# Attention with decay and a mixture of experts on one core: the decay of a second block moved to TensorE, a fetch moved ahead of the last features, and a new table of steps

## The chip, the cores and the metric

One core of a Trainium2 chip runs the whole program in one launch. The metric is device time in microseconds (us), the median of several runs. The engines are named as in the profile: PE is TensorE (PEld its weight loads), DVE is VectorE, ACT is ScalarE, POOL is GpSimd, SP is SyncE, whose queue issues most DMAs.

## The reference

Attention with a causal mask and a decay from cumulated gates, then a mixture of 8 experts, of which each row uses one:

```python
scores = (1 / sqrt(D)) * q @ k.T                  # B=8, H=8, S=576, D=64
cum = cumsum(log(clip(f, 1e-4, 1)))
scores = where(causal, -1e9, scores + cum[:, None] - cum[None, :])
attn = exp(scores - max(scores)); attn /= sum(attn) + 1e-9
x = (attn @ v).transpose(...).reshape(4608, 512)
e = argmax(x @ w_gate)                            # one expert for each row
out[row] = gate * sigmoid(x @ w_output_gate)[e] * (relu(x @ w1[e]) @ w2[e])
```

## The kernel before, in words

**Attention** works on 32 pairs of heads (u = 0 to 31), both heads of a pair side by side on the partitions. A row's maximum is found ahead of its scores, by a product of 16-bit halves in four parts (`maxsteps`): the full block (rows 384 to 511, 512 columns), a mixed part (the third block, 384 columns, and the first, 128), the second block (rows 128 to 255, 256 columns) and the rest (the last 64 rows of both heads). All four write the one PSUM tile `mx`, so each product waits until DVE has reduced the part before it. From pair 2 on, the decay of all blocks but the first is not in the product: a DVE operation (L294, `CUSTOM_DVE_ANT_0`, one for each head) adds it from the tile `wide` and takes the maximum. Where the decay is in the product (`Eq`, `Ek`), a plain reduction (L279) is enough.

The maxima are turned on PE (`mt`), copied to rows (`mts`, L353) and stored into `Eq` by DMA (`max_put`). Then PE makes the scores `sc` in three groups for each head, ACT takes the exponentials (L378, tile `p`), and the rest of each exponential against its 16-bit part is a subtract (`plo`, L380) on POOL. PE multiplies `p` and `plo` with the values (`av`), DVE and ACT normalise (L483 to L499). Other subtracts of the same kind are those of the values V (`Vs`, L124 called from `load_v`: part 0 on POOL, part 1 on DVE) and of the features (`feats`, L124 and L523 on DVE). All these DVE subtracts have both inputs in SBUF.

**Routing** (`route`) runs for one batch, that is four pairs, at a time: a product `lg`, a chain of small DVE operations, ranks `rk`, and then 4 or 5 indirect DMAs that scatter rows into the table (`tbl`, L643) on POOL. A batch with an odd number has 5 tiles, one with an even number 4. `hold_early` (L549 to L552) reserves places of an early expert; it uses the same PSUM bank as `mt`, `lg`, `rk` and the rest's scores `rs`.

**Order.** All of attention is issued in an order written out by the table `OFF`: the loop of `attention()` counts steps s, six to a pair; each kind of work has an offset there, and `order` says in which order the kinds of one step are issued. Each engine works through its own queue in that order. `'hold'` has the steps of `hold_early`, `'v'` those of `load_v`, `'first'` the step of the first pair's maxima.

**Experts.** For each, W1 and W2 come in 8 pieces each by DMA (`fetch_w1`, `fetch_w2` on SP's queue) and are split into a 16-bit part (ACT) and a rest; `up_products` makes `hp` (L909), `up_split` its two halves (L918, L919), `down` makes `y` (L937 to L939). The first expert begins with three tiles of rows that are known early. In its loop over fc, the features of the last batch half (`feats(NQ - 1)`) are cast, subtracted, transposed by DMA and stored.

Of the kernel before, what the change touches and what calls it, by code (L numbers as in the profile page):

```python
# [50 lines left out]

OFF = {'lead': 3, 'crow': -12, 'clear': 33, 'clearstep': 12, 'prefill': -12, 'fetch': -21, 'spread': -19, 'end': 204, 'max': (-15, -13, -11, -10), 'pair': -8, 'mturn': -7, 'rows': -6, 'put': -4, 'rscore': 2, 'rexp': 3, 'first': -9, 'av': ((6, 8, 8), (9, 10, 10)), 'fetch_v': -24, 'v': ((-16, -8, -15), (-10, -1, -17)), 'feats0': 20, 'feats1': 22, 'fturn': 22, 'fturnstep': 2, 'fout': 32, 'route': 46, 'rank': 6, 'w1r': [169, 170, 171, 175, 176, 177, 181, 182], 'w1': [174, 175, 176, 179, 181, 183, 185, 187], 'w2r': [183, 184, 185, 186, 187, 188], 'hold': (160, 188), 'ids1': 192, 'gather': 172, 'ids': 7, 'gturn': 6, 'route_last': 200, 'nsum': (9, 11), 'nrec': (10, 12), 'nx': (10, 13), 'nrest': (11, 14), 'mv': ['xr', 'v0', 'sm'], 'begin': -18, 'wg': -4, 'fetch_v/1': -10, 'dve': [181, 183, 185, 187, 189, 191], 'w1pool': [0, 1, 2, 3, 4, 5, 6, 7], 'order': 'scores put nrec reduce max spread tick feats1 rows v0 nsum fout nx tick v1 fetch_v feats0 exps extra pair tick mturn av rexp fturn nrest fetch route rscore tick maxrest'}
MV = OFF['mv']
ENGINES = {mybir.EngineType.PE, mybir.EngineType.Activation, mybir.EngineType.DVE, mybir.EngineType.Pool,
           mybir.EngineType.SP}
# [7 lines left out]
def _attn_moe(ctx, tc, qk, vm, f, wg, w1, w2, out):  # L65
    nc = tc.nc
# [8 lines left out]
    crow = dr.tile([3, B * H, S], F16, name="crow")  # L75
# [76 lines left out]
    order = actx.enter_context(ExitStack())  # L152
# [101 lines left out]
    def maxsteps(u):  # L254

        t = st[u]
        Ku, Qu = upper(t["K"]), upper(t["Q"])
        nR = t["nR"] = a.tile([P, NW], F32, name="nR", bufs=3)
        w = HU * NC
        nW = nR[:, 0:w].rearrange("p (i c) -> p i c", i=HU)  # L260

        def few(x, i, sl):

            return x[i * D:(i + 1) * D - 1, sl]

        def block(m, o, c):
            n = (c + 1) * P
            q = slice(c * P, n)
            decay = [(lambda i: part(m, i, o, n), lambda i: few(t["Eq"], i, q), lambda i: few(t["Ek"], i, slice(0, n)),
                      False, False)]  # L270
            return [(lambda i: part(m, i, o, n), lambda i: Qu[rows(i), q], lambda i: Ku[rows(i), 0:n], True, False),
                    *([] if "wide" in t and c else decay),
                    (lambda i: part(m, i, o + n - P, P), lambda i: pick[rows(i), 0], lambda i: negm[rows(i), 0],
                     False, False),
                    (lambda i: part(m, i, o + n - D, D), lambda i: pick[rows(i), 1], lambda i: negm[rows(i), 1, D:],
                     False, True)]

        def red(o, x):
            nc.vector.tensor_reduce(o, x, axis=AX.X, op=ALU.max)  # L279

        def part(m, i, o, n):
            return m[i][:, o:o + n] if isinstance(m, list) else m[:, i, o:o + n]

        def most(m, o, c):
            n = (c + 1) * P
            if "wide" not in t or not c:
                if isinstance(m, list):
                    for i in range(HU):
                        red(nW[:, i, c:c + 1], part(m, i, o, n))
                else:  # L290
                    red(nW[:, :, c], m[:, :, o:o + n])
                return
            for i in range(HU):
                nc.vector.tensor_tensor_reduce(out=spare[:, 0:n], in0=part(m, i, o, n), in1=t["wide"][:, i * S:i * S + n],  # L294
                                               scale=1.0, scalar=-3e38, op0=ALU.add, op1=ALU.max,
                                               accum_out=nW[:, i, c:c + 1])

        def mtile():
            return ps.tile([P, 2, 512], F32, name="mx", bufs=1)

        def full():
            m = mtile()
            heads(block(m, 0, 3))
            yield
            most(m, 0, 3)

        def mixed():
            m = [ps.tile([P, 512], F32, name="av", bufs=2) for _ in range(HU)] if u < 2 else mtile()
            heads(block(m, 0, 2))
            heads(block(m, 384, 0))  # L310
            yield
            most(m, 0, 2)
            most(m, 384, 0)

        def second():
            m = [ps.tile([P, 512], F32, name="sc", bufs=3) for _ in range(HU)] if u < 1 else mtile()
            heads(block(m, 0, 1))
            yield
            most(m, 0, 1)

        def rest():
            m = mtile().rearrange("p b n -> p (b n)")[:, 0:S]
            q = slice(SM, S)
            for sl in (slice(0, SM), q):
                own = sl is q
                heads([(lambda i: m[rows(i), sl], lambda i: Qu[rows(i), q], lambda i: Ku[rows(i), sl], True, False),
                       (lambda i: m[rows(i), sl], lambda i: few(t["Eq"], i, q), lambda i: few(t["Ek"], i, sl),
                        False, not own)])
            heads([(lambda i: m[rows(i), q], lambda i: pick[rows(i), 0, 0:SR], lambda i: negm[rows(i), 0, 0:SR],
                    False, True)])  # L330
            yield
            red(nR[:, w:w + 1], m)

        return [full(), mixed(), second(), rest()]
# [316 lines left out]
    NF = FF // P  # L651
# [15 lines left out]
    W1, W1r, W2r = [], {}, []  # L667

    def fetch_w2(we, fc):
        raw = ar.tile([P, DM], F32, name="w2r", bufs=6)  # L670
        nc.sync.dma_start(raw, we[fc])
        return raw
# [194 lines left out]
    def split_w2(raw, eng):  # L867
        h = m2.tile([P, DM], F16, name="w2h", bufs=16)
        l = m2.tile([P, DM], BF16, name="w2l", bufs=16)
        nc.scalar.copy(out=h, in_=raw)  # L870
        eng.tensor_tensor(l, raw, h, op=ALU.subtract)
        return h, l
# [29 lines left out]
    def up_products(w1s, x, tiles, fc):  # L902
        xT = x[1]
        wh, wl = w1s[fc]
        hp = [pm.tile([P, 512], F32, name=f"hp{j}", bufs=2) for j in range(len(tiles))]
        for k in range(ND):
            for i, (w, j) in enumerate(((wh, 0), (wh, 1), (wl, 0))):
                for m, (t0, t1) in zip(hp, tiles):
                    nc.tensor.matmul(m[:, 0:(t1 - t0) * P], w[:, k], xT[:, t0:t1, k // 2, j, k % 2],  # L909
                                     start=k == 0 and i == 0, stop=k == ND - 1 and i == 2)  # L910
        return hp

    def up_split(hp, h, tiles, fc):
        hh, hl = h
        for m, (t0, t1) in zip(hp, tiles):
            sl = slice(t0 * P, t1 * P)
            m = m[:, 0:(t1 - t0) * P]
            nc.scalar.activation(out=hh[:, fc, sl], in_=m, func=AF.Relu)  # L918
            nc.vector.scalar_tensor_tensor(hl[:, fc, sl], m, 0.0, hh[:, fc, sl],  # L919
                                           op0=ALU.max, op1=ALU.subtract)  # L920
# [41 lines left out]
    x = st["early"]  # L962
    x1 = (st["ids"], m2.tile([P, CT, 2, 2, DM // P // 2, P], F16, name="xT", bufs=1))
    first = [(0, ET)]
    late_rows = [(ET, CT)]
    with tc.manual_schedule(engines=ENGINES):
# [3 lines left out]
        h = hidden()  # L970
        W2, W1b, W2b = [], [], []
        for fc in range(NF):
            if fc == 1:
                for part in range(2):
                    feats(NQ - 1, part)
                    for t in ((0,), (2, 4))[part]:
                        feats_turn(NQ - 1, t)
                feats_out(NQ - 1)
            up_split(up_products(W1, x, first, fc), h, first, fc)
            W2.append(split_w2(W2r[fc], nc.vector))  # L980
            if len(W2r) < NF:
                W2r.append(fetch_w2(w2[0], len(W2r)))
        W1r = [fetch_w1(m2, w1[1], fc, 8) for fc in range(NF)]
        for t in range(ET):
            gather_turn(x1, t, (ET + t) % CT)
        W2r = [fetch_w2(w2[1], fc) for fc in range(6)]
# [36 lines left out]
        W2r = [fetch_w2(w2[EE], fc) for fc in range(6)]  # L1023
# [9 lines left out]
        W2 = []  # L1033
# [11 lines left out]
        W1, x = W1c, x2  # L1045

        halves = [(0, CT // 2), (CT // 2, CT)]
        for e in range(EE, E):
# [9 lines left out]
            h = hidden()  # L1058
# [8 lines left out]
            if more:  # L1067
                W2r = [fetch_w2(w2[e + 1], fc) for fc in range(6)]
# [5 lines left out]
            if more:  # L1074
                W1, W2, x = W1n, W2n, xn

    with tc.For_i(0, nsl, 1) as i:
# [4 lines left out]
        x = gather(m2, tbl[bass.ds(bi, P)], 1)  # L1082
        h = up(weights(load_w1, w1[bass.ds(ei, 1)].rearrange("a f p k n -> (a f) p k n")), x, [(0, 1)])
# [46 lines left out]
```

## Time and profile before

| | |
|---|---|
| median of 3 runs | 808.67 us (808.04 to 808.94) |
| profiled execution | 803.02 us, span 801.3 us |
| granted TensorE clock, mean over the span | 0.976 |
| PE busy | 749.1 us (93%), 8635 products |
| POOL busy | 483.9 us (60%) |
| DVE busy | 368.9 us (46%) |
| ACT busy | 341.8 us (43%) |
| custom max operations (L294) on DVE | 100.0 us, 180 rows |
| DMA | 121.44 MB, 152 GB/s |

The table is a whole-span mean over stages. Attention fills about the first 371 us, where DVE's and POOL's busy shares in slices are mostly 0.7 to 0.9; the experts fill the rest, where PE is busy without a break and DVE is mostly idle. A timeline row gives the start, the duration, the engine, the line, the operation with output and inputs, how many were merged, and in brackets the idle time before it with what ended it.

### The profile page before, as it was taken

The page shows a single profiled execution, that of the slowest core. Times are in us where ns is not written, and L with a number is a line of the kernel's source. Part 1 is how long each engine was busy: PE and PEld are TensorE (multiplying, and loading weights), DVE is VectorE, ACT ScalarE, POOL GpSimd, SP SyncE. Part 2 cuts the span into 40 slices and gives each one's busy share as a digit, 9 for nine tenths or more (in the row PEclk, how much of TensorE's full clock was granted, in tenths as well). Part 3 has the DMA queues.
Part 4 walks back from the last instruction along what each step waited for, and adds up shares of the span by engine and source line. Part 5 has one row for each costly group of instructions (what it writes and reads, how often), then busy time and mean ns, then how long its engine had stood idle before and what let it go on. Part 6 is the DMA issues. An engine that isn't in the chain of part 4 may idle for free. (4 is left out here: it accounts for less than half of the span.)

```text
span 801.3 us, 21234 instructions
## 1 busy us (share of the span) xinstructions
PE 749.1 (93%) x8635; PEld 489.4 (61%) x8635; DVE 368.9 (46%) x982; ACT 341.8 (43%) x817; POOL 483.9 (60%) x505
## 2 busy tenths in 40 slices
PE   3899998999899989979799999999999999999996
PEld 2577776776577667657354667557466474564752
DVE  7576787787778886795352152102011020120210
ACT  2456664565455563565342434324233233333211
POOL 9768787797768786684162477464473654736001
PEclk9999999999899998998899999999999999999998
DMA  5546669788877976699956929458462593542001
GB/s 184 168 128 167 179 156 148 182 173 180 141 168 172 155 172 138 146 181 199 210 162 148 285 85 228 135 178 182 159 143 94 172 215 101 154 126 80 10 14 44
DMA packets 136180, 121.44 MB, mean 152 GB/s; under 512 B 95310, under 2 KB 104910, under 8 KB 136080
## 3 DMA queue, kind: packets, MB, share of 16 engines
q1 hardware_dynamic: 128528, 101.14, 55.3%
q0 software_dynamic: 7552, 18.92, 7.9%
q8 instruction: 68, 1.11, 0.6%
q14 instruction: 32, 0.26, 0.2%
HBM read 81.63 MB, written 20.48 MB: 127 GB/s over the span
## 5 line engine op out<-in xcount | busy, mean ns | idle before, releaser
L380 POOL TENSOR_TENSOR plo<-p 128x512 f16<-128x512 f32 x186 | 194.3, 1057 | 77.4 <-ACT p L378 74.7
L919 DVE SCALAR_TENSOR_TENSOR hl<-hp,hh 128x384 f16<-128x384 f32 (+1 forms) x128 | 60.8, 491 | 296.4 <-ACT hh L918 296.4
L909 PE MATMUL hp<-xT,w1h 128*128 128x256 f16 (+1 forms) x1024 | 188.0, 299 | 0.1
L378 ACT ACTIVATE p<-sc 128x512 f32<-128x512 f32 x192 | 110.6, 594 | 61.4 <-PE sc L252 60.7
L252 PE MATMUL sc<-qk 64*128 64x64 f32 (+5 forms) x642 | 131.8, 480 | 0.0
L942 POOL DMA_INDIRECT out_dram<-ys,ids x40 | 40.2, 1004 | 143.6 <-ACT ys L941 97.3
L294 DVE CUSTOM_DVE_ANT_0 spare<-mx,wide 128x512 bf16<-128x512 f32 (+1 forms) x180 | 100.0, 556 | 57.5 <-PE mx L252 54.3
L937 PE MATMUL y<-w2h,hh 128*128 128x512 f16 x320 | 122.3, 382 | 4.2 <-ACT w2h L870 4.2
L909 PEld LDWEIGHTS <-w1h 128*128 128x128 f16 x1024 | 100.1, 98 | 40.5 <-issue 0.3
L938 PE MATMUL y<-w2l,hh 128*128 128x512 bf16 x320 | 122.1, 382 | 0.1
L939 PE MATMUL y<-w2h,hl 128*128 128x512 f16 x320 | 122.1, 382 | 0.0
L909 PE MATMUL hp<-xT,w1l 128*128 128x384 f16 (+1 forms) x512 | 121.9, 299 | 0.0
L918 ACT ACTIVATE hh<-hp 128x384 f16<-128x384 f32 (+1 forms) x128 | 50.7, 435 | 121.5 <-PE hp L909 120.6
L941 ACT ACTIVATE ys<-y,ids 128x512 f32<-128x512 f32 x40 | 27.5, 687 | 152.2 <-issue 94.7
L663 POOL TENSOR_TENSOR w1l<-w1r,w1h 128x512 bf16<-128x512 f32 x52 | 59.5, 1156 | 47.2 <-ACT w1h L662 42.6
L252 PEld LDWEIGHTS <-pick 64*128 64x128 bf16 (+1 forms) x1152 | 59.4, 98 | 41.9 <-issue 25.2
L252 PE MATMUL mx<-qk 64*64 64x64 bf16 (+2 forms) x374 | 57.2, 310 | 27.5 <-DVE nR L279 14.6
L452 PE MATMUL av<-Vs,p 128*128 128x65 f16 x640 | 72.0, 196 | 2.5 <-ACT xr L499 2.5
L454 PE MATMUL av<-Vs,plo 128*128 128x65 f16 x640 | 70.9, 194 | 0.5 <-POOL plo L380 0.5
L453 PE MATMUL av<-Vs,p 128*128 128x64 bf16 x640 | 71.3, 197 | 0.0
L452 PEld LDWEIGHTS <-p 128*128 128x128 bf16 x640 | 59.5, 98 | 7.4 <-issue 0.5
L453 PEld LDWEIGHTS <-p 128*128 128x128 bf16 x640 | 60.8, 99 | 2.4 <-issue 2.4
(158 smaller groups left out, 1404.0 us busy)
## 6 DMA issues: line engine op xcount, KB each, us to landing
qk<-in_qk_dram SPq DMA_DIRECT2D x32, 576.0 KB
w1r<-in_w_dram SPq DMA_DIRECT2D x64, 256.0 KB
w2r<-in_w_dram SPq DMA_DIRECT2D x64, 256.0 KB
v<-in_vm_dram SPq DMA_DIRECT2D x16, 576.0 KB
wide<-crow SPq DMA_DIRECT2D x30, 288.0 KB
xbuf<-x SPq DMA_DIRECT2D x16, 512.0 KB
Eq<-mts SPq DMA_DIRECT2D x64, 0.1 KB
xbuf<-x SPq DMA_DIRECT2D x16, 64.0 KB
```

Of the source, the lines that this page charges most:

```text
L252: nc.tensor.matmul(dst(i), w(i), x(i), start=start, stop=stop)
L294: nc.vector.tensor_tensor_reduce(out=spare[:, 0:n], in0=part(m, i, o, n), in1=t["wide"][:, i * S:i * S + n], scale=1.0, scalar=-3e38, op0= ...
L378: nc.scalar.activation(out=f32, in_=src, func=AF.Exp, scale=0.125)
L380: eng.tensor_tensor(lo, f32, upper(f32), op=ALU.subtract)
L452: nc.tensor.matmul(dst, ph, vv[:, 0:W], start=kc == 0, stop=False)
L453: nc.tensor.matmul(dst[:, 0:D], ph, vv[:, W:].bitcast(BF16), start=False, stop=False)
L454: nc.tensor.matmul(dst, pl, vv[:, 0:W], start=False, stop=kc == qc)
L909: nc.tensor.matmul(m[:, 0:(t1 - t0) * P], w[:, k], xT[:, t0:t1, k // 2, j, k % 2], start=k == 0 and i == 0, stop=k == ND - 1 and i == 2)
L919: nc.vector.scalar_tensor_tensor(hl[:, fc, sl], m, 0.0, hh[:, fc, sl], op0=ALU.max, op1=ALU.subtract)
L937: nc.tensor.matmul(y, hh[:, fc, sl], wh, start=fc == 0, stop=False)
L938: nc.tensor.matmul(y, hh[:, fc, sl], wl, start=False, stop=False)
L939: nc.tensor.matmul(y, hl[:, fc, sl], wh, start=False, stop=fc == NF - 1)
```

## The change

The decay of the second block (c = 1) goes into the product on PE for all pairs, and its maximum is one plain reduction over both heads in place of two custom operations. In the first expert, the last features are handled after the second round of the loop (products, splits and the fetch of W2's next piece) in place of before it. And the table has other offsets and another order within a step.

```diff
-OFF = {'lead': 3, 'crow': -12, 'clear': 33, ... 'prefill': -12, 'fetch': -21, 'spread': -19, ... 'put': -4, ... 'first': -9, 'av': ((6, 8, 8), (9, 10, 10)), 'fetch_v': -24, 'v': ((-16, -8, -15), (-10, -1, -17)), ... 'fturn': 22, ... 'hold': (160, 188), ... 'fetch_v/1': -10, ... 'order': 'scores put nrec reduce max spread tick feats1 rows v0 nsum fout nx tick v1 fetch_v feats0 exps extra pair tick mturn av rexp fturn nrest fetch route rscore tick maxrest'}
+OFF = {'lead': 3, 'crow': -16, 'clear': 32, ... 'prefill': -14, 'fetch': -21, 'spread': -20, ... 'put': -5, ... 'first': -7, 'av': ((6, 7, 8), (10, 10, 10)), 'fetch_v': -25, 'v': ((-15, -9, -18), (-9, 0, -14)), ... 'fturn': 21, ... 'hold': (160, 197), ... 'fetch_v/1': -14, ... 'order': 'spread nrec reduce scores tick rows put feats0 max tick v1 feats1 fetch_v nsum v0 exps extra mturn nx pair fout route tick fetch av nrest rexp rscore fturn tick maxrest'}
...
-                    *([] if "wide" in t and c else decay),
+                    *([] if "wide" in t and c > 1 else decay),
...
-            if "wide" not in t or not c:
+            if "wide" not in t or c < 2:
...
         for fc in range(NF):
+            up_split(up_products(W1, x, first, fc), h, first, fc)
+            W2.append(split_w2(W2r[fc], nc.vector))
+            if len(W2r) < NF:
+                W2r.append(fetch_w2(w2[0], len(W2r)))
             if fc == 1:
                 for part in range(2):
                     feats(NQ - 1, part)
                     for t in ((0,), (2, 4))[part]:
                         feats_turn(NQ - 1, t)
                 feats_out(NQ - 1)
-            up_split(up_products(W1, x, first, fc), h, first, fc)
-            W2.append(split_w2(W2r[fc], nc.vector))
-            if len(W2r) < NF:
-                W2r.append(fetch_w2(w2[0], len(W2r)))
```

What the table moves, at three places. On DVE, around the subtracts of V's part 1 (`Vs`), in a group of four pairs in the middle of attention; before:

```order
L294 ISA spare,nR<-mx,wide 128x512
L294 ISA nR 128x1
L124 TENSOR_TENSOR x_4697<-x,x_4697 128x2x256
L124 TENSOR_TENSOR x_4697<-xr,x_4697 128x256
L492 TENSOR_TENSOR x<-av,sm 128x4x64
L124 TENSOR_TENSOR Vs_90<-v_3852,Vs_90 128x9x64
L488 RECIPROCAL sm<-sm 128x5
L294 ISA spare,nR<-mx,wide 128x384
```

and now:

```order
L279 TENSOR_REDUCE nR<-mx 128x2
L353 COPY mts<-mt 9x128
L124 TENSOR_TENSOR Vs_90<-v_3850,Vs_90 128x9x64
L492 TENSOR_TENSOR x<-av,sm 128x4x64
L279 TENSOR_REDUCE nR<-mx 128x2
L279 TENSOR_REDUCE nR<-mx 128x1
L124 TENSOR_TENSOR Vs_91<-v_4378,Vs_91 128x9x64
L488 RECIPROCAL sm<-sm 128x5
L294 ISA spare,nR<-mx,wide 128x512
```

The first of the two stood between the full block's maxima (512 columns) and the mixed part's (384); now it stands behind the mixed part's, the second (before: behind the second block's maxima) behind the rest's (`128x1`).

On POOL, the scatters (`tbl`) of a four-tile routing among the subtracts of exponentials; the last two scatters and what follows them before:

```order
L643 DMA tbl<-rec,pi 36864x2
L380 TENSOR_TENSOR plo<-p_4902 128x512
L380 TENSOR_TENSOR plo<-p_4938 128x512
L394 TENSOR_TENSOR prl_94<-prf_93 128x128
L643 DMA tbl<-rec,pi 36864x2
L380 TENSOR_TENSOR plo<-p_4902 128x512
L380 TENSOR_TENSOR plo<-p_4938 128x512
L380 TENSOR_TENSOR plo<-p_5141 128x512
L380 TENSOR_TENSOR plo<-p_5178 128x512
```

and now:

```order
L643 DMA tbl<-rec,pi 36864x2
L380 TENSOR_TENSOR plo<-p_4960 128x512
L394 TENSOR_TENSOR prl_94<-prf_93 128x128
L380 TENSOR_TENSOR plo<-p_4920 128x512
L643 DMA tbl<-rec,pi 36864x2
L380 TENSOR_TENSOR plo<-p_4960 128x512
L380 TENSOR_TENSOR plo<-p_5161 128x512
L380 TENSOR_TENSOR plo<-p_5201 128x512
```

Both scatters come one subtract later; one subtract of the same pair, not two, is left behind the last.

On PE, the product of `hold_early` at its second use, near the end of attention; before, it stood between the scores of the last pair and the products of values:

```order
L252 LDWEIGHTS Ek_81
L252 MATMUL sc<-Eq_86,Ek_81 128x64
L549 LDWEIGHTS ones_205
L549 MATMUL hold<-runs,ones_205 128x1
L452 LDWEIGHTS p_8049
L452 MATMUL av<-Vs_90,p_8049 128x65
```

and now behind the last products of values, ahead of a routing's first product:

```order
L465 MATMUL av<-Vs_90,prl_96 128x65
L549 LDWEIGHTS ones_205
L549 MATMUL hold<-runs,ones_205 128x1
L564 LDWEIGHTS xT_7340
L564 MATMUL lg<-wgs,xT_7340 128x32
```

Before, the last pair's rest scores (`rs`) came after it in the same PSUM bank; now the routing's `lg` does.

## Rows read from the trace of the kernel before

**Rows 1.** Windows: us, busy us of each engine, granted clock (PEclk), DMA share, GB/s.

```profile
212.70:219.50 6.80, 5.85 (x72) 4.30 (x72) 3.73 (x12) 1.29 (x5) 3.61 (x5) 0.50 0.93 110
359.50:366.30 6.80, 6.21 (x87) 5.15 (x88) 2.31 (x8) 2.11 (x7) 2.16 (x3) 0.50 1.07 209
393.60:400.50 6.90, 5.53 (x51) 2.57 (x51) 3.19 (x9) 3.37 (x6) 0.99 (x1) 0.51 1.27 298
```

**Rows 2.** Waits of PE, whole span: us in total, times, longest us.

```profile
PE mx L252 <- DVE nR L279: 14.6, 8, 3.0
PE mx L252 <- DVE nR L294: 7.9, 15, 1.4
```

**Rows 3.** Timeline of PE, first score product of some pairs.

```profile
206.35 1.13 PE L252 MATMUL sc<-qk 64*128 64x512 f32 x4
...
221.92 1.13 PE L252 MATMUL sc<-qk 64*128 64x512 f32 x4
...
252.73 1.13 PE L252 MATMUL sc<-qk 64*128 64x512 f32 x4
...
262.35 1.13 PE L252 MATMUL sc<-qk 64*128 64x512 f32 x4
...
274.33 1.13 PE L252 MATMUL sc<-qk 64*128 64x512 f32 x4
```

**Rows 4.** Timeline of PE and DVE at a second block; the last row from the start.

```profile
225.65 0.28 PE L252 MATMUL mx<-qk 64*128 64x256 bf16 x2
225.77 0.25 PE L252 MATMUL mx<-negm,pick 64*128 64x128 bf16 x4
...
226.06 0.42 DVE L294 CUSTOM_DVE_ANT_0 spare<-mx,wide 128x256 bf16<-128x256 f32 x1 [0.26 <-PE mx L252]
...
226.88 0.69 DVE L124 TENSOR_TENSOR x<-x,x 128x512 f16<-128x512 f32 x1
...
19.66 0.69 DVE L279 TENSOR_REDUCE nR<-mx 128x2 f32<-128x512 f32 x1
```

**Rows 5.** Timeline of DVE, POOL and PE at subtracts of V's part 1.

```profile
208.15 3.96 DVE L124 TENSOR_TENSOR Vs<-v,Vs 128x576 bf16<-128x576 f32 x1
...
208.44 3.04 POOL L380 TENSOR_TENSOR plo<-p 128x512 f16<-128x512 f32 x3
...
213.65 0.39 PE L252 MATMUL mx<-qk 64*128 64x256 bf16 x2 [3.00 <-DVE nR L279]
...
254.20 0.74 DVE L124 TENSOR_TENSOR Vs<-v,Vs 128x576 bf16<-128x576 f32 x1
```

**Rows 6.** Timeline of POOL, DVE and PE in a pair without scatters.

```profile
61.47 2.04 POOL L380 TENSOR_TENSOR plo<-p 128x512 f16<-128x512 f32 x2 [0.25 <-ACT p L378]
...
62.76 0.40 DVE L492 TENSOR_TENSOR x<-av,sm 128x256 f32<-128x256 f32 x1
...
64.74 0.40 PE L252 MATMUL mx<-qk 64*64 64x512 bf16 x2
```

**Rows 7.** Timeline of DVE, POOL and PE at a subtract of the features.

```profile
267.30 3.61 DVE L124 TENSOR_TENSOR x<-x,x 128x512 f16<-128x512 f32 x1
...
267.31 3.04 POOL L380 TENSOR_TENSOR plo<-p 128x512 f16<-128x512 f32 x3
...
271.63 0.40 PE L252 MATMUL mx<-qk 64*128 64x512 bf16 x2 [1.60 <-DVE nR L279]
```

**Rows 8.** Timeline of PE, the last pair's rest scores.

```profile
360.09 0.48 PE L252 MATMUL rs<-qk 64*64 64x64 f32 x4 [3.23 <-DVE late L550]
```

**Rows 9.** Timeline of SP's queue and PE in the first expert.

```profile
384.35 0.54 SPq L671 DMA_DIRECT2D w2r<-in_w_dram x1
...
394.83 0.58 PE L937 MATMUL y<-w2h,hh 128*128 128x512 f16 x1 [4.24 <-ACT w2h L870]
```

**Rows 10.** Timeline of DVE at the start, the second pair's full reduction.

```profile
16.83 1.23 DVE L279 TENSOR_REDUCE nR<-mx 128x2 f32<-128x1024 f32 x1 [0.43 <-PE mx L252]
```

More of the change, by code (lines that the diff above doesn't have):

```diff
@@ L50 @@
 EE = 2
-OFF = {'lead': 3, 'crow': -12, 'clear': 33, 'clearstep': 12, 'prefill': -12, 'fetch': -21, 'spread': -19, 'end': 204, 'max': (-15, -13, -11, -10), 'pair': -8, 'mturn': -7, 'rows': -6, 'put': -4, 'rscore': 2, 'rexp': 3, 'first': -9, 'av': ((6, 8, 8), (9, 10, 10)), 'fetch_v': -24, 'v': ((-16, -8, -15), (-10, -1, -17)), 'feats0': 20, 'feats1': 22, 'fturn': 22, 'fturnstep': 2, 'fout': 32, 'route': 46, 'rank': 6, 'w1r': [169, 170, 171, 175, 176, 177, 181, 182], 'w1': [174, 175, 176, 179, 181, 183, 185, 187], 'w2r': [183, 184, 185, 186, 187, 188], 'hold': (160, 188), 'ids1': 192, 'gather': 172, 'ids': 7, 'gturn': 6, 'route_last': 200, 'nsum': (9, 11), 'nrec': (10, 12), 'nx': (10, 13), 'nrest': (11, 14), 'mv': ['xr', 'v0', 'sm'], 'begin': -18, 'wg': -4, 'fetch_v/1': -10, 'dve': [181, 183, 185, 187, 189, 191], 'w1pool': [0, 1, 2, 3, 4, 5, 6, 7], 'order': 'scores put nrec reduce max spread tick feats1 rows v0 nsum fout nx tick v1 fetch_v feats0 exps extra pair tick mturn av rexp fturn nrest fetch route rscore tick maxrest'}
+OFF = {'lead': 3, 'crow': -16, 'clear': 32, 'clearstep': 12, 'prefill': -14, 'fetch': -21, 'spread': -20, 'end': 204, 'max': (-15, -13, -11, -10), 'pair': -8, 'mturn': -7, 'rows': -6, 'put': -5, 'rscore': 2, 'rexp': 3, 'first': -7, 'av': ((6, 7, 8), (10, 10, 10)), 'fetch_v': -25, 'v': ((-15, -9, -18), (-9, 0, -14)), 'feats0': 20, 'feats1': 22, 'fturn': 21, 'fturnstep': 2, 'fout': 32, 'route': 46, 'rank': 6, 'w1r': [169, 170, 171, 175, 176, 177, 181, 182], 'w1': [174, 175, 176, 179, 181, 183, 185, 187], 'w2r': [183, 184, 185, 186, 187, 188], 'hold': (160, 197), 'ids1': 192, 'gather': 172, 'ids': 7, 'gturn': 6, 'route_last': 200, 'nsum': (9, 11), 'nrec': (10, 12), 'nx': (10, 13), 'nrest': (11, 14), 'mv': ['xr', 'v0', 'sm'], 'begin': -18, 'wg': -4, 'fetch_v/1': -14, 'dve': [181, 183, 185, 187, 189, 191], 'w1pool': [0, 1, 2, 3, 4, 5, 6, 7], 'order': 'spread nrec reduce scores tick rows put feats0 max tick v1 feats1 fetch_v nsum v0 exps extra mturn nx pair fout route tick fetch av nrest rexp rscore fturn tick maxrest'}
 MV = OFF['mv']
```

## The prediction

> **What bounds the kernel now.** I read the stretches with their granted clock first, then the waits of PE, then the timeline of single engines. The median of the runs shown is 808.67 us; the profiled execution took 803.02 us, 5.65 us less, and its span is 801.3 us. All durations below come from that execution, the sum is made against its 803.02 us, and the 5.65 us are added at the end.
>
> PE is the engine that sets the pace (93% of the span busy), so what counts is when PE waits, and how fast it runs behind a wait. The waits view says where: in the attention stage PE waits 14.6 us for plain reductions of the maxima on DVE and 7.9 us for the combined add-and-max operations there [rows 2]. Behind the longest of these waits (one of three stands in the rows), and behind two others near the end of attention and in the first expert, the granted clock is 0.50 or 0.51 for almost 7 us, that is the lower level of 1.2 GHz [rows 1]. So a wait of 3 us costs more than 3 us.
>
> The work repeats by pair of heads. One pair lasts 9.6 us from its first score product to the next (252.73 to 262.35) when nothing waits, 11.98 us in a pair where a wait of 1.6 us falls (262.35 to 274.33), and 15.57 us in one where the wait of 3.0 us falls (206.35 to 221.92) [rows 3]. Three pairs are of the last kind and two of the middle one.
>
> Why the 3.0 us: DVE's subtract for the values of V (part 1) took 3.96 us instead of 0.74 [rows 5]. POOL began a train of three subtracts 0.29 us after it, and DVE's ended 0.63 us after the train. Behind it stood the reductions that free the maxima's buffer, so PE's product of the second block waited. A DVE subtract with both inputs in SBUF that meets POOL's subtracts is thus held for the whole train. The features' subtract shows the same thing: 3.61 us, beside another train of three, then a PE wait of 1.60 us [rows 7].
>
> **The change part by part.**
>
> *Decay of the second block.* PE gets two more products of 128x256 in each of 30 pairs. Products of that size, also one for each head, take 0.12 us of PE's time (225.65 to the next at 225.77) [rows 4]: 3.6 us if all 30 pairs are bound by PE. On DVE two operations of 0.82 us together (226.06 to 226.88) become one of 0.69 us (the same shape stands at 19.66) [rows 4]. Where PE waited for these two (the waits view counts 15 such waits on their line, of which I take two as waits for the other blocks) [rows 2], in 13 of the 30 pairs, the pair gets 0.13 us shorter, and the products lie inside the wait; in the other 17 the 0.12 us show. 17 x 0.12 - 13 x 0.13 = +0.3 us (bounds -1.7 to +3.6).
>
> *V's part 1 on DVE.* It leaves the place ahead of the mixed block's reductions. That takes away the three long pairs: 15.57 - 9.62 = 5.95 us here [rows 3]; the first of the three has a shorter slow stretch, so I take **-17 us** for all. Its two new places: one right behind the copy of the maxima's rows, ahead of a product of values and the second block's reduction; one behind the last block's reduction, where the next reduction is over 1 us away and nothing is queued that PE waits for, so nothing. For the first place, in the two pairs without table scatters, POOL's train ends at 61.47 + 2.04 = 63.51; plus 0.63 for the subtract, 0.40 for the product and 0.69 for the reduction that is 65.2, where PE comes at 64.74 + 0.12 = 64.86 [rows 4, 5, 6]. V's cast now also stands ahead of two exponentials, which makes the train later. I take 0.7 us, twice: +1.4 us. In five pairs with scatters, POOL's order has a scatter exactly there, and beside a scatter this subtract took 0.74 us [rows 5]: I take 0, with bounds 0 and 5.95 us each.
>
> *The features' subtract* keeps its place on DVE, but the scatters move back by one subtract, so POOL comes later into the next pair. Behind the three four-tile routings, I count four subtracts in the train over it where two to three stood; behind the two five-tile ones a scatter now parts the train. One subtract is 3.04 / 3 = 1.0 us [rows 7]. So the wait becomes 1.6 + 1.0 = 2.6 us three times, and 0.6 us twice: 9.0 against 3.2 us before, +5.8 us. The clock fell behind waits of 3.0 us and not behind 1.6; for 2.6 I count half of the three, at 5.95 - 3.0 = 2.9 us each: +4.4 us. Together **+10.2 us** (bounds -3.2, no wait at all, and +14.5, all three slow).
>
> The Trainium skill speaks against the length of these waits: "SBUF — State Buffer", section "Who interferes with whom", says that the shared port pair is held for one instruction, and the other engine blocks until that one ends. By that a blocked DVE subtract would lose one POOL subtract, not three. The trace disagrees twice [rows 5, 7], so the sum goes by the trains; what it would be by the rule is the third rival.
>
> *The start.* The first pair's maxima are now turned and stored behind the next pair's full reduction (1.23 us) [rows 10], and V's first subtract slips in between the first reductions (0.7 us). The first scores wait for that store: +1.9 us (bounds 0 and 4; some may hide in the DMA's flight).
>
> *The early-place hold* (the operation that reserves rows for an early expert) moves from between two score steps to behind the last products of values. PE loses the 3.23 us wait for it [rows 8], and the slow stretch behind it, 6.21 us of PE work at half clock [rows 1], of which 2.5 to 3.1 us go. Next late are the last exponentials' subtracts on DVE, which the wait covered; I leave 0.5 us for them. **-5.2 us** (bounds -2.7 and -6.3).
>
> *The last features behind the weight fetch.* The eighth piece of W2 was issued at 384.35, behind three transposes and the stores of the features, and PE waited 4.24 us for it at 394.83 [rows 9], again with a slow stretch of 5.53 us of work at 0.51 [rows 1], worth 2.4 us. With the fetch ahead of the transposes it is issued some 9 us earlier, more than the wait. SP's queue behind the transposes gets hardly later, but PE comes 6 us sooner to the second expert, whose transposed rows are last in it: 0.5 us back. **-6.1 us** (bounds -3 and -6.6). The features' route is read only after a first tile of the down products, so its two steps later cost nothing.
>
> Sum: 0.3 - 17 + 1.4 + 10.2 + 1.9 - 5.2 - 6.1 = -14.5 us, 788.5 us for the profiled execution; with 5.65 us, **794 us**. The expert stage behind it has no PE wait and only shifts.
>
> **The rivals.**
> - *Slower: V's subtract is caught in its first new place.* If POOL has finished the scatter and begun its three subtracts when DVE gets there, each of five pairs has the 3.0 us wait with its slow stretch: 5 x 5.95 = 29.8 us, 794 + 30 = **824 us**. It decides when POOL is over a microsecond further than I count. For it: POOL's lead of only 0.29 us decided before [rows 5]. Against: POOL is behind, not ahead, in these pairs. Chance 0.10.
> - *Only the end gains.* New trains cost what the old ones did, so the middle gives nothing: 0.3 + 1.9 - 5.2 - 6.1 = -9.1, **800 us**. For it: the total of POOL's work is the same, and the three 2.6 us waits may all turn slow. Chance 0.25.
> - *The trains part.* A DVE subtract gets in after one POOL subtract, for whatever reason: POOL less behind, or the pair of ports handed over. Then the features' wait goes too, since the reduction behind it has 3.61 - 1.60 = 2.0 us to spare: 0.3 - 17 + 0 - 3.2 + 1.9 - 5.2 - 6.1 = -29.3, **779 us**. Against it: the two rows with whole trains; for it: POOL's lag is only counted, and a train that is parted by an exponential's lateness gives the same. It is also what the rule of the Trainium skill's page "SBUF — State Buffer" would do here. Chance 0.15.
> - *The fetch is not what was late.* If W2's piece lands late for the traffic beside it and not for its issue, the 6.1 us stay: **800 us**. For it: it took almost 10 us from issue to use; against: half of that traffic, W1's fetch, comes behind it either way. Chance 0.05.
>
> **How the numbers follow.** My forecast has 0.45. 794 us is its time. Its own bounds run from 783 to 806; the range takes in the rivals at 800 and the one at 779, and leaves out 824: 779 to 806. A measurement of this kernel can tell about 0.2%, 1.6 us. All but the first rival are faster by more; I leave 0.02 for landing within it: faster 0.88, same 0.02, slower 0.10.
>
> **What would show it.** No PE wait for W2 near the first down products, and none for the hold; no pair of 15.6 us in the old places; V's subtract at 0.7 to 1.5 us. The weak step is the features' subtract: rows of 3 to 4 us on it in pairs behind a four-tile routing, with PE waits of 2.6 us, confirm it; rows near 0.7 mean the third rival. A V subtract of 3 us or more behind the copy of the rows means the first. A start longer by more than 4 us, or slow stretches in new places, would make the prediction wrong.

## The result, and the profile after

The change took 798.51 us (median of 10 runs, 794.49 to 804.26) beside 807.84 us for the kernel before on the same chip (10 runs, 804.61 to 810.59). The ratio is 0.9895, 95% interval 0.9871 to 0.9919, that is 8.5 us less (6.5 to 10.4). The forecast was 794 us, a fall of 14.5.

The profiled executions are less far apart: 800.09 us after, with a span of 798.4 us, against 803.02 us. The one of before lies below all ten of its runs here, the one of after among its own. So the profiles tell where time went, and the ratios how much it was. The mean granted clock of the span went from 0.976 to 0.984.

The waits of PE after (us in total, times, longest), whole span, to be held against [rows 2]:

```profile
PE mx L252 <- DVE nR L279: 8.2, 9, 1.7
...
PE hp L909 <- DVE hl L919: 3.6, 2, 2.8
PE av L452 <- ACT xr L499: 3.4, 4, 1.1
PE hp L909 <- issue: 3.3, 1, 3.3
PE sc L252 <- DMA Eq<-mts: 2.1, 3, 1.1
...
PE sc L252 <- issue: 1.4, 1, 1.4
...
PE mx L252 <- DVE nR L294: 0.5, 2, 0.4
...
PE lg L564 <- DVE late L550: 0.3, 1, 0.3
```

The waits for plain reductions fell from 14.6 to 8.2 us with none above 1.7, those for the combined operations from 7.9 to 0.5, and that for the hold from 3.23 [rows 8] to 0.3; the one for W2 [rows 9] is gone. New are waits of `sc` for the maxima's store (`Eq<-mts`; the one of 1.4 us stands before the same product, with no releaser named) and of `hp` in the experts.

The timeline of DVE, POOL, SP and PE after, at the places of [rows 3, 5, 7]:

```profile
134.84 3.60 DVE L124 TENSOR_TENSOR x<-x,x 128x512 f16<-128x512 f32 x1
...
139.16 0.40 PE L252 MATMUL mx<-qk 64*128 64x512 bf16 x2 [1.38 <-DVE nR L279]
...
178.84 1.52 DVE L124 TENSOR_TENSOR x<-x,x 128x512 f16<-128x512 f32 x1
...
209.19 0.87 DVE L124 TENSOR_TENSOR Vs<-v,Vs 128x576 bf16<-128x576 f32 x1
209.59 1.32 POOL L643 DMA_INDIRECT tbl<-rec,pi  x1 [0.17 <-issue]
...
264.88 3.04 POOL L380 TENSOR_TENSOR plo<-p 128x512 f16<-128x512 f32 x3
266.06 2.42 DVE L124 TENSOR_TENSOR x<-x,x 128x512 f16<-128x512 f32 x1
...
297.80 0.36 SPq L96 DMA_DIRECT2D v<-in_vm_dram  x1
298.21 0.62 SPq L358 DMA_DIRECT2D Eq<-mts  x1
...
305.73 0.39 PE L252 MATMUL sc<-Eq,Ek 64*128 64x512 f16 x2 [1.11 <-DMA Eq<-mts]
```

V's subtract in its first new place takes 0.87 to 1.09 us in the five pairs with scatters. The scatters come in groups of four (pairs 10 to 11, 18 to 19, 26 to 27) and of five (14 to 15, 22 to 23). In pairs 15 and 23 the features' subtract takes 1.52 and 2.42 us, not 3.6: the fifth scatter now ends the train. Behind the groups of four it takes 3.60 us in pair 11, and 1.06 and 0.68 us in pairs 19 and 27. The store of the maxima stands right behind the fetch of `v` (576 KB), and PE waits for it 7.5 us after its issue.

With the pairs counted from 0 and a pair's length taken from its first score product to the next one's, as in [rows 3], the middle compares so:

| pairs | before | after | term of the prediction: forecast, measured |
|---|---|---|---|
| 10, 18, 26 (V's subtract) | 14.64, 15.57, 15.82 | 9.95, 10.22, 10.31 | -17, **-15.6** |
| 2, 6 (V's first new place) | 9.42, 9.47 | 9.80, 10.26 | +1.4, **+1.2** |
| 11, 19, 27 (features, four-tile routing) | 10.40, 10.40, 10.41 | 13.66, 16.02, 12.02 | +12.2, **+10.5** |
| 15, 23 (features, five-tile routing) | 11.97, 11.98 | 11.23, 10.71 | -2.0, **-2.0** |
| 12, 16, 24 (the pairs behind those) | 10.05, 10.01, 10.00 | 10.73, 11.47, 11.56 | none, **+3.7** |
| 15 others (decay, one reduction) | | | +0.3, **-3.7** |
| first two pairs (start of pair 2) | 40.45 | 40.66 | +1.9, **+0.2** |

(The features' +10.2 is 3 x 2.6 + 4.4 in the three pairs and 2 x (0.6 - 1.6) in the two.) Together -5.7 us up to pair 30 (341.60 before, 335.94 after), where the terms gave -3.2. From there to the end of the span it is 459.7 us before and 462.5 us after: the end, forecast at -11.3, gave nothing in these two executions. One execution says little here: the stretch lasts 459.7 to 466.9 us in the seven profiles of this document with the end as before, and 458.2 to 464.1 in the five with both edits of it. Its rows after:

```profile
372.31 1.01 SPq L671 DMA_DIRECT2D w2r<-in_w_dram  x2
...
379.50 0.49 ACT L918 ACTIVATE hh<-hp 128x384 f16<-128x384 f32 x1 [4.44 <-remote]
...
380.64 0.48 PE L909 MATMUL hp<-xT,w1h 128*128 128x384 f16 x1 [3.33 <-issue]
...
442.94 0.27 PE L909 MATMUL hp<-xT,w1h 128*128 128x256 f16 x1 [2.85 <-DVE hl L919]
```

W2's last fetch leaves at 372.9 in place of 384.35 [rows 9], as foreseen. But PE now stands 3.3 us within the first expert's products, and 2.85 us more at the second's.

And the windows (columns as in [rows 1]) with half the clock:

```profile
219.60:226.40 6.80, 6.22 (x74) 4.49 (x71) 3.78 (x10) 3.22 (x8) 4.07 (x4) 0.50 0.59 170
356.20:363.00 6.80, 5.72 (x107) 5.60 (x105) 3.02 (x8) 2.63 (x8) 3.13 (x4) 0.50 1.11 184
```

The first is pair 19, behind the waits for `Eq`; the second is the old stretch at the hold [rows 1], which stayed although the hold's wait went: waits for ACT's `p` (1.42 us) and `xr` (1.08 us) stand there now. Two shorter ones, of 3.4 us, begin at 141.1 and 380.1.

### The profile page after: what moved, and what is told of

It is laid out like the page before. It is cut to its first block, busy times and chain, and to the rows that moved or that the text cites. A ratio compares the mean times of both kernels' runs of the same rounds, so it can differ in the third digit from the quotient of the medians.

```text
span 798.4 us, 21224 instructions
## 1 busy us (share of the span) xinstructions
PE 753.5 (94%) x8676; PEld 496.5 (62%) x8695; DVE 349.9 (44%) x892; ACT 341.7 (43%) x817; POOL 483.1 (61%) x505
## 5 line engine op out<-in xcount | busy, mean ns | idle before, releaser
L252 PE MATMUL sc<-qk 64*128 64x64 f32 (+5 forms) x642 | 135.3, 476 | 1.4 <-ACT p L378 1.4
L938 PE MATMUL y<-w2l,hh 128*128 128x512 bf16 x301 | 114.1, 379 | 0.0
L294 DVE CUSTOM_DVE_ANT_0 spare<-mx,wide 128x512 bf16<-128x512 f32 (+1 forms) x120 | 74.6, 622 | 50.5 <-PE mx L252 46.2
L252 PEld LDWEIGHTS <-pick 64*128 64x128 bf16 (+1 forms) x1152 | 61.4, 97 | 38.2 <-issue 20.4
L279 DVE TENSOR_REDUCE nR<-mx 128x1 f32<-128x576 f32 (+3 forms) x95 | 60.5, 637 | 32.8 <-PE mx L252 32.4
L252 PE MATMUL mx<-qk 64*64 64x64 bf16 (+2 forms) x374 | 58.4, 303 | 14.5 <-DVE nR L279 8.2
L452 PEld LDWEIGHTS <-p 128*128 128x128 bf16 x640 | 60.0, 99 | 7.4 <-issue 1.4
```

Of the source, the lines that this page charges most:

```text
L252: nc.tensor.matmul(dst(i), w(i), x(i), start=start, stop=stop)
L452: nc.tensor.matmul(dst, ph, vv[:, 0:W], start=kc == 0, stop=False)
L938: nc.tensor.matmul(y, hh[:, fc, sl], wl, start=False, stop=False)
```

## The experiments

Each was timed against the kernel before on its own chip. In us, a ratio is taken of 807.84.

**V's subtracts alone.**

```diff
 # before
-'v': ((-16, -8, -15), (-10, -1, -17))
+'v': ((-15, -9, -18), (-9, 0, -14))
```

> The kernel before with one edit: only the steps of the subtracts of V ('v') are those of the change. Theory A (the prediction's): V's part-1 subtract was held by POOL's trains, and away from them the three pairs of 14.6 to 15.8 us become pairs of about 10, so the time falls by 17 - 1.4 = about 15 us; the two pairs of 12.0 us with the features' subtract stay as they are. Theory B (from the profile after): the subtract now releases the buffer of v later than the maxima are ready, the fetch of v stands ahead of the maxima's store in SP's queue, and the pair after the long one waits for that store; the fall is then some 17 - 11 = 6 us, with waits of sc for Eq in the pairs next to the old long ones. Theory C: the three long pairs are not V's doing and stay, 0 us.

Measured: ratio 1.0067 (1.0042 to 1.0091), **5.4 us slower**. All three theories missed the time; theory B's wait for `Eq` comes in one pair (2.46 us in pair 11). The profile is of the slowest of this kernel's 12 runs (816.69 us; median 811.06). The timeline of this kernel, at pair 10 and pair 22:

```profile
126.44 3.99 DVE L124 TENSOR_TENSOR Vs<-v,Vs 128x576 bf16<-128x576 f32 x1
...
126.77 3.03 POOL L380 TENSOR_TENSOR plo<-p 128x512 f16<-128x512 f32 x3
...
260.14 1.05 POOL L380 TENSOR_TENSOR plo<-p 128x512 f16<-128x512 f32 x1
...
260.25 2.84 DVE L124 TENSOR_TENSOR x<-x,x 128x512 f16<-128x512 f32 x1
...
263.82 0.19 PE L452 MATMUL av<-Vs,p 128*128 128x65 f16 x1 [1.50 <-ACT xr L499]
```

V's subtract is caught once in its new place, as my slower rival had it. In pairs 14, 18, 22 and 26 the features' subtract, 0.69 us where no train runs and 1.5 us at this place before, is caught instead (2.84 to 3.44 us), and the normalisation behind it makes PE wait 1.5 to 2.0 us; the four pairs last 11.9 to 15.1 us.

**The decay alone.**

```diff
 # before
-*([] if "wide" in t and c else decay),
+*([] if "wide" in t and c > 1 else decay),
...
-if "wide" not in t or not c:
+if "wide" not in t or c < 2:
```

> The kernel before with the second block's decay on TensorE and its one reduction, nothing else. Theory A (the prediction's term): +0.3 us, bounds -1.7 to +3.6: 0.12 us more in pairs without a wait, some 0.13 us less in pairs with one; the three long pairs stay. Rival: the waits of PE for the combined add-and-max operations, 7.9 us in the profile before and 0.5 us in the profile after, go with this edit, and the time falls by 4 us or more. A third: DVE, shorter by 0.13 us in each pair, reaches V's subtract earlier, ahead of POOL's train, and the long pairs go: -10 us or more.

Measured: 1.0123 (1.0073 to 1.0172), **9.9 us slower**. The three long pairs are five: pairs 14 and 22 grew from 9.62 to 14.9 and 15.2. The timeline of POOL, DVE and PE at pair 14:

```profile
165.72 1.25 POOL L643 DMA_INDIRECT tbl<-rec,pi  x1 [0.17 <-issue]
...
166.37 4.29 DVE L124 TENSOR_TENSOR Vs<-v,Vs 128x576 bf16<-128x576 f32 x1
...
167.00 3.04 POOL L380 TENSOR_TENSOR plo<-p 128x512 f16<-128x512 f32 x3
...
172.20 0.39 PE L252 MATMUL mx<-qk 64*128 64x256 bf16 x2 [3.19 <-DVE nR L279]
```

The same place where the decay is as before (from the kernel with the two edits of the end, below):

```profile
166.06 1.25 POOL L643 DMA_INDIRECT tbl<-rec,pi  x1 [0.17 <-issue]
...
166.71 0.74 DVE L124 TENSOR_TENSOR Vs<-v,Vs 128x576 bf16<-128x576 f32 x1
...
167.33 3.04 POOL L380 TENSOR_TENSOR plo<-p 128x512 f16<-128x512 f32 x3
```

By the traces POOL's train begins as long after the subtract's start in the one (0.624 us) as in the other (0.623), and the subtract takes 4.29 and 0.74 us. So these pairs stood on an edge that a trace can't resolve, and behind this edit both fell on the other side. (Pair 14 of the second kernel lasts 14.06 us all the same, by a wait of PE of 3.88 us with no releaser named.) PE's waits for the combined operations (7.9 us before) went to 1.4, much as the first rival had it, but that was outweighed.

**V's part 1 on POOL.**

```diff
 # before
-'mv': ['xr', 'v0', 'sm']
+'mv': ['xr', 'v0', 'v1', 'sm']
```

> The kernel before with V's part-1 subtract on POOL in place of DVE, at the same step. Theory A (DVE's subtract is held by POOL's trains, and that makes the three pairs of about 15 us): DVE has nothing there to be held, the three pairs become some 10 us, and the time falls by 10 to 16 us, less than 17 because POOL has 1.25 us more in every second pair and the features' subtract may meet longer trains. Theory B (POOL is what PE waits for in truth, DVE's long row is only a sign of it): the pairs stay long, with waits for plo or for the reductions, and the time is within 5 us of before or above it.

Measured: 1.0067 (1.0042 to 1.0092), **5.4 us slower**. The three pairs became 9.97, 9.81 and 9.85 us, as theory A had it, while the time is in theory B's range. But POOL is now later, and the features' subtract takes the place of V's: pairs 15 and 23 grew to 16.6 us, 11, 19 and 27 to 12.7, 13.3 and 16.1. The timeline of DVE and POOL at pair 15, and PE's waits:

```profile
176.50 5.02 POOL L380 TENSOR_TENSOR plo<-p 128x512 f16<-128x512 f32 x5
...
176.58 6.85 DVE L124 TENSOR_TENSOR x<-x,x 128x512 f16<-128x512 f32 x1
...
181.49 0.39 POOL L394 TENSOR_TENSOR prl<-prf 128x128 f16<-128x128 f32 x1
181.84 1.03 POOL L380 TENSOR_TENSOR plo<-p 128x512 f16<-128x512 f32 x1
```

```profile
PE mx L252 <- DVE nR L279: 16.0, 8, 4.5
```

DVE's subtract spans seven subtracts of POOL and ends 0.56 us after the last of them (183.43 against 182.87). That a DVE subtract can be held through many subtracts of POOL is thereby shown a second way. The Trainium skill ("SBUF — State Buffer", section "Who interferes with whom") says that a DVE instruction with two SBUF inputs contends with POOL's reads, which this trace bears out; its rule that the port is held for one instruction, read so that the waiting engine goes next, would end the wait after one subtract of 1.03 us, which the row of 6.85 us does not bear out.

**The table without the decay, and the middle without the end.** The first is the new table with the old hold, decay and features; the second has the decay too. The second was timed twice.

```diff
 # after (both kernels)
-'hold': (160, 197)
+'hold': (160, 188)
...
 # and the last features ahead of the second round again; in the first kernel also
-*([] if "wide" in t and c > 1 else decay),
+*([] if "wide" in t and c else decay),
```

> The new table without the decay on TensorE, the hold and the features as before. By the prediction (+0.3 us for the decay) 3.5 us less than before, within 1 us of the decay and table together. Theory B (from the decay alone, 9 us slower, and V's steps alone, 4.6 us slower): the table fits only the shorter DVE work of the new reduction; without it a subtract meets a train in two to four more pairs, and the time is 4 to 15 us above that of decay and table together.

> The kernel after the change with both edits of the end undone: the decay and the new table alone. By the prediction's terms 0.3 - 17 + 1.4 + 10.2 + 1.9 = 3.2 us less than before. By the difference of what was measured for the change (9.3 us) and for the end alone (5.2 us) 4 us less. A rival: the middle does nothing of itself, 0 us, and the two edits of the end gain more behind the new middle than behind the old one.

> The decay and the new table alone once more, since the first timing of it spread over 16 us. If middle and end add up, the middle is worth the change's 8.5 us less the end's 5.8 us, about 3 us less than before. If they do not (the end's two edits are worth little behind the new middle, because the same later waits set its length), the middle alone is worth 7 to 9 us, as the first timing had it.

Measured: the table 0.9956 (0.9926 to 0.9986), -3.6 us; table and decay 0.9896 (0.9843 to 0.9948) and 0.9891 (0.9855 to 0.9927), **-8.4 and -8.8 us**. So the middle alone is worth as much as the whole change (-8.5), within some 3 us, more than the first timing's expectation had (-3.2 or -4) and in the 7 to 9 us that the second's had for the case that middle and end don't add. The decay, 9.9 us slower behind the old table, is some 5 us faster behind the new one (-8.4 against -3.6), as theory B of the first had it at its lower bound: its cost hangs on where the subtracts stand. In the new table PE's waits for the combined operations go with it (6.7 us with the table alone, 0.5 with both), and V's subtract isn't there to be caught.

**The store ahead of the fetch.**

```diff
 # after
-'fetch_v': -25
+'fetch_v': -23
```

> The kernel after the change with the fetch of v two steps later in the table, so that it stands behind the maxima's store in SP's queue and not ahead of it. Theory B (the new wait of the change is that store behind the fetch): the waits of PE for Eq in the pairs of 13.7, 16.0 and 12.0 us go, these pairs become about 10 us (13.7 keeps up to 1.5 us for the features' subtract), and the time falls by some 8 to 11 us against the change, to about 788 to 790 us. Rival: Eq lands late from the other traffic (transposes, scatters), whatever stands ahead of it in the queue: within 2 us of the change. A second rival: v itself lands too late for its subtracts, and the time rises.

Measured: 0.9875 (0.9833 to 0.9916), -10.1 us against -8.5 for the change; the intervals overlap, so the two are not told apart. The waits for `Eq` are gone from the three pairs, which shows that the place in SP's queue made them. But the pairs became 13.39, 12.84 and 15.56 us, in sum 41.79 against 41.70: taking the waits away did not shorten them. Theory B's 8 to 11 us did not come; the time is that of the first rival, though not for its reason. The timeline of SP, DVE and PE around pair 27:

```profile
292.92 0.35 SPq L235 DMA_DIRECT2D wide<-crow  x1
...
295.44 0.50 SPq L96 DMA_DIRECT2D v<-in_vm_dram  x1
297.18 4.25 SPq L531 DMA_TRANSPOSE xT<-x  x1
...
301.02 0.69 DVE L294 CUSTOM_DVE_ANT_0 spare<-mx,wide 128x512 bf16<-128x512 f32 x1 [2.15 <-DMA wide<-crow]
...
302.51 0.34 PE L252 MATMUL mx<-qk 64*128 64x384 bf16 x2 [1.45 <-DVE nR L294]
```

A transpose behind the fetch holds SP's queue for 4.25 us (1.31 us in the change). The last fetch of `wide` ahead left at 292.92, but DVE's combined operation has its tile only at 301.02, and PE waits 1.45 us for that. In pair 11 PE waits 0.85 us for `qk`, and in pair 19 the features' subtract meets a train, takes 4.35 us, and PE waits 1.31 us behind it. The wait moved among transfers and trains.

**The end: both edits, and each alone.**

```diff
 # before
-'hold': (160, 188)
+'hold': (160, 197)
...
 # and the last features behind the fetch of W2, as in the change
```

> The kernel before with the two edits of the end alone: the hold behind the last products of values, and the last features behind the weight fetch. Theory A (the prediction's): 5.2 + 6.1 = 11.3 us less than before, with neither the PE wait of 3.2 us for the hold nor that of 4.2 us for W2. Theory B (from the profile after, whose end gained only a few us less than its middle): other stalls in the first expert take the place of the two waits, and the fall is 0 to 4 us.

> The kernel before with the hold moved behind the last products of values, nothing else. Theory A (the prediction's term): 5.2 us less, bounds 2.7 and 6.3; the 3.2 us wait for the hold and its slow stretch go, 0.5 us for other late work stays. Theory B (from the profile with both edits of the end, where PE waits 2.9 us for ACT's xr in the same place): the next late work, hidden by the hold before, takes most of the wait, and the fall is 1 to 3 us.

> The kernel before with the last features behind the weight fetch, nothing else. Theory A (the prediction's term): 6.1 us less, bounds 3 and 6.6; no PE wait for W2. Theory B (from the profile with both edits): the wait for W2 goes, but the routing's first product then waits some 1.6 us for the features' transposes and the second expert's first product up to 2.9 us for its rows, and the fall is 1 to 4 us.

Measured: both 0.9928 (0.9901 to 0.9955), **-5.8 us**; the hold 0.9985 (0.9959 to 1.0010), -1.2; the features 0.9968 (0.9936 to 1.0000), -2.6. Theory B holds for both parts, though the hold alone is not told apart from nothing, and with both edits the fall is above its 0 to 4. PE's waits with the hold moved alone:

```profile
PE y L937 <- ACT w2h L870: 6.3, 1, 6.3
...
PE av L452 <- ACT xr L499: 4.6, 5, 2.9
```

With the features moved alone:

```profile
PE hp L909 <- DVE hl L919: 2.9, 2, 1.8
PE hp L909 <- DMA xT<-xg: 2.8, 1, 2.8
...
PE rk L606 <- DVE oh L592: 1.8, 1, 1.8
```

Where the hold's wait of 3.23 us was, there is one of 2.9 for ACT's rest of the values. PE reaches the first expert 1.7 us sooner (26.73 in place of 28.48 us after pair 30's start), and the wait for W2, which comes when its transfer does, grows from 4.24 to 6.3 us. It is 0.6 to 8.9 us in the other profiles that have the end as before, so one profile doesn't show that it took what the hold gave. With the features later, W2's wait goes, and waits for the routing's chain, the splits and the second expert's rows come.

**Fetch, features, products.** Two kernels, the second with the store ahead of the fetch as well.

```diff
 # after, in the loop over fc
-up_split(up_products(W1, x, first, fc), h, first, fc)
 W2.append(split_w2(W2r[fc], nc.vector))
...
     feats_out(NQ - 1)
+up_split(up_products(W1, x, first, fc), h, first, fc)
```

> The kernel after the change, with the first expert's loop written so that W2's split and the fetch of its next piece stand first, then the last features, then the products: the fetch is still ahead of the features' transposes, and the transposes are issued one round (about 2 us) sooner. Theory A (the features' lateness cost the waits of the routing's products and of the second expert's rows): 1 to 4 us less than the change, without PE waits for lg or rk in the first expert. Rival (these waits and the stalls behind them come from DMA traffic that is the same in both): within 2 us of the change. Second rival: ACT's and DVE's work for the features comes ahead of the splits of the products again, and PE waits for hl: 1 to 3 us more.

> The change with both edits, the fetch of v behind the maxima's store and W2's fetch, features, products in that order. If both help as told for each alone, 3 to 6 us less than the change, about 793 to 795 us; if the waits only move among transfers, within 2 us of it.

Measured: 0.9896 (0.9872 to 0.9920) and 0.9882 (0.9851 to 0.9912), -8.4 and -9.5 us: both the same as the change, by the rivals. PE's waits in the first of them:

```profile
PE sc L252 <- DMA Eq<-mts: 5.0, 2, 3.7
...
PE lg L564 <- DMA xT<-x: 3.6, 2, 2.3
```

The routing's product still waits for the transposes, though they are issued a round earlier. Its attention is that of the change, and pairs 11, 19 and 27 wait there again (14.02, 17.26, 12.00 us): these waits recur. No kernel here beats the change by more than its interval.

## Why the prediction was right, and where it was not

The direction, the range (779 to 806) and the place of the main gain were right. The time was 4.5 us above the forecast and the fall 8.5 us in place of 14.5, and the sum hid errors of opposite sign: by ratios the middle gave -8.4 to -8.8 us where its terms gave -3.2, and the end behind it about 0, within some 3 us, where its terms gave -11.3. That the time came out so near is partly luck.

- **V's subtract, -17 us: right in size** (-15.6), cause shown (the row of 3.96 us is 0.87, and with the subtract on POOL the three pairs are short as well). What failed is that I priced it as if it could be had alone. Without the rest of the table the train catches another subtract.
- **Its first new place, +1.4: right** (+1.2) for PE and DVE. "I take 0" for the five pairs with scatters is right for the engines and failed for a queue: this subtract frees the buffer that the next fetch of `v` needs. SP waits there for it (2.98 us at 207.1 to 210.1 in the change), and the maxima's store stands behind. I had costed what waits on DVE and PE for it, and not what waits on SP. In the change's profile the waits for that store (0.72, 1.35 and 1.11 us in pairs 11, 19 and 27), with the slow stretch behind the second, are the larger part of these pairs' +10.5 us. But without them the three pairs are as long (41.79 us), so the store is not all that sets their length.
- **The features' subtract, +10.2: near in size** (+10.5 - 2.0 = +8.5 in its five pairs), **for the forecast's reason only in part**. Behind the five-tile routings a scatter parted the train as foreseen. Behind the four-tile ones "I count four subtracts in the train" came true in pair 11 (a train of five, 3.60 us), with a PE wait of 1.38 us where 2.6 was forecast. In pairs 19 and 27 the subtract met no such train, and the waits for the store stand there instead; that the size fits is luck. With the store ahead of the fetch it is pair 19 that has the subtract at 4.35 us and a PE wait of 1.31. The term left out the pairs behind (+3.7). "The clock fell behind waits of 3.0 us and not behind 1.6" doesn't hold either: in the change stretches at 0.50 follow waits of 1.35 and 1.42 us.
- **The decay, +0.3: failed** (-3.7 in 15 pairs; -0.8 with the table alone, so -2.9 by the decay). "The pair gets 0.13 us shorter" took the second operation's time off a wait that stays; in pairs 9, 13, 17 and 21 the wait of 0.69 us went to 0.32 to 0.34 by the table alone, and to nothing with the decay as well. Pairs without a wait got 0.12 us longer, as foreseen.
- **The start, +1.9: too high** (+0.2). Pair 2 begins at 40.3 to 41.5 us in the seven profiles with the new table, and at 40.3 to 41.3 in six with the old one and its steps for V's part 1.
- **The hold, -5.2: failed** (-1.2 alone). "I leave 0.5 us" for what is late next was 2.9 us, and the slow stretch behind the wait stayed. Where the rest went is not shown: W2's wait was longer in that profile, but it differs as much between profiles with the same end.
- **The features behind the fetch, -6.1: failed** (-2.6 alone). The fetch was what was late: no profile with this edit has a wait for W2, which is 4.2 to 8.9 us in all others but one, so the fourth rival is out. But "two steps later cost nothing" and "0.5 us back" failed: in the change, 0.28 + 3.33 + 0.78 + 2.85 = 7.2 us of waits stand between the last products of values and the second expert's first products, and 4.2 to 7.5 us in the other profiles with the edit.
- **The rivals.** "Only the end gains" (800 us) is closest in time and the wrong way round: in the change the middle gains. "The trains part" (779 us) has the time wrong, but its mechanism is found: in the change's pair 6 V's subtract got in after the first of three subtracts of POOL (rows at the end). So "held for the whole train", read from [rows 5, 7], is not a rule for every train. The slower rival's mechanism is real (3.99 us at pair 10 with V's steps alone), but the rest of the table keeps POOL off that place.

Open: why the end's edits, worth -5.8 us behind the old middle, show no gain behind the new one. By the intervals up to some 3 us could hide there, and the profiles from pair 30 on differ by more than that with the same end. Open too is what keeps pairs 11, 19 and 27 at 41.7 us or more in sum in every profile with the new table (31.2 before): waits for the store, for `wide`, for the transposes, for ACT and behind the features' subtract take turns there, and no run here isolated them.

## What to carry to other kernels

When the subtracts of two engines hold each other up and one engine runs in trains, a stall belongs to the train and not to the instruction that is caught: moving that instruction, alone or to the other engine, let the next one be caught, and only an order fitted as a whole gained. When a step moves, follow the buffer it frees to the queue that waits for it, and see what stands behind that wait; but time the kernel without that wait before calling it the cause, since another may stand ready. Gains need not add: -8.4 to -8.8 us and -5.8 us made -8.5 together.

## What the hardware showed beyond that

- Which of the two engines is held goes, in these profiles, with what POOL comes from more than with a head start. Over all 14 profiles, between 40 and 360 us, 122 DVE subtracts began up to 0.54 us ahead of a subtract of POOL that found POOL idle: none was held (0.67 to 0.76 us), and POOL's took up to 2.15 us in place of 1.05. Where POOL came from an indirect DMA, 29 of 38 were held (1.67 to 4.29 us), with leads up to 0.70 us; at 0.62 us both occur. In the kernel before, the subtract of [rows 5] with a lead of 0.29 us was held behind the first row here; that of [rows 4] at 226.88, with 0.14 us, was not, and the second row, 2.04 us for two subtracts in [rows 6], took 2.43:

```profile
207.17 1.25 POOL L643 DMA_INDIRECT tbl<-rec,pi  x1 [0.17 <-issue]
...
227.02 2.43 POOL L380 TENSOR_TENSOR plo<-p 128x512 f16<-128x512 f32 x2 [0.87 <-ACT p L378]
```

- A train isn't always run out. In the change's pair 6, V's subtract began within the first of three POOL subtracts without a gap and ended 0.61 us after that first one (at 83.20); the three took 3.55 us in place of 3.04. What lets it in is not shown:

```profile
82.16 3.55 POOL L380 TENSOR_TENSOR plo<-p 128x512 f16<-128x512 f32 x3 [1.17 <-ACT p L378]
...
82.52 1.29 DVE L124 TENSOR_TENSOR Vs<-v,Vs 128x576 bf16<-128x576 f32 x1
```

- In some executions PE falls behind without a wait that the profile names. In the change ACT's `hh`, which waits for a batch of PE's products, starts 4.44 us late at 379.50 and 3.43 us late at 442.05, released by something that the profile does not tell ("remote"), though PE's rows of these batches, whose ends the profile models, end at 377.31 and 440.10 us at the latest; PE then waits for the split behind it. The profile of before has nothing of the kind at these places, four others have PE waits of 1 to 2.8 us at the second. Which input was lacking wasn't found.
